# Fewer conversion steps in late slots, and another order of the integer additions, in a threshold-attention and GELU-MLP kernel

## The chip, the cores and the metric

The kernel runs on one core of one Trainium2 chip. The metric is the device time of one execution in microseconds, and the median over runs is what counts. Before the change it is 1330.39 us (three runs, 1327.67 to 1331.37).

## The reference

Attention runs over 8 batches of 8 heads, with 576 positions of 64 features, all in fp32. An MLP with exact GELU follows on the 4608 rows of 512.

```python
scores = scale * np.matmul(q, k.transpose(0, 1, 3, 2))
thresh = np.max(scores, axis=-1, keepdims=True) - tau
scores = np.where(scores >= thresh, scores, -1000000000.0)
scores = scores - np.max(scores, axis=-1, keepdims=True)
attn = np.exp(scores)
attn = attn / (np.sum(attn, axis=-1, keepdims=True) + 1e-09)
attn_out = np.matmul(attn, v)
# (B,H,S,D) -> (B*S, H*D)
h = x @ w_in                                      # 512 -> 2048
g = 0.5 * h * (1.0 + erf(h * inv_sqrt2))
out = g @ w_out                                   # 2048 -> 512
```

## The kernel before

Two heads form a pair; there are 32 pairs, four to a batch. The 576 rows of a head are cut into four chunks of 128 rows and a tail of 64. The tails of both heads of a pair share one chunk, chunk 4, which has one score tile instead of two. The main loop runs over slots `n`, each with one chunk `i` of one pair `p`. Slots 0 to 7 take chunks 0 and 1 of pairs 0 to 3. Slots 8 to 19 take chunks 2, 3 and 4 of these pairs in turn, so slots 10, 13, 16 and 19 are the one-chunk slots. From slot 20 on each pair has five slots in a row. Each engine's instructions run in the order in which the code issues them; semaphores between tiles do the rest.

A slot does this, for each head `e` of its pair:
- `scores` (L432, PE): scores into a PSUM tile `sc`, of which there are two buffers, so that the scores of the next slot wait until the last step below has read this slot's.
- `softmax_head`: the negated row maximum `nmx` (L444, DVE), the threshold `thr` (L447, GpSimd), and the exponential `p` (L449, ACT).
- `softmax_tail`: `p` where the score reaches the threshold, with the row sums (L465, DVE).
- Beside it PE does the transposes of `p` (L373), `weigh_v` (L603, L635) and, from slot 10, first steps of the MLP (L703).

While slots 1 to 21 run, the weights are rewritten. They come in 32 pieces of 128x512 words, 16 of `w_in` and 16 of `w_out`, and a pipeline of three engines converts each. `convert_first` takes two ACT instructions (L200, L201), one piece ahead. `convert_second` takes two DVE instructions, L208 (shift and mask) and L209 (sign bit), and then asks for the load of a later piece (L184, on the SP queue). `add_low_bits` takes one integer addition on GpSimd (L220), which makes the piece usable by PE. `STEPS[n]` says how many pieces slot `n` converts, at its end. Their additions are due in the next slot, at two places: one in `softmax_head`, after the first `nmx` is issued and ahead of `thr`, and the rest after `softmax_head`. In the kernel before, the first of these takes the newest of the sums that are due, and the second takes all that are left, oldest first.

The slot's other GpSimd work includes the divisions of early pairs. `divide_late` (L509, two multiplications) is issued in the slots that `DIVIDE_LATE` lists, behind the additions. At the end of slots 18 and 19 DVE transposes k and q of pair 4 (L410, L415) for the scores of slot 20. Slot 17 sets part of a `v` tile to zero on GpSimd (L256).

At the start, `load_early` loads q and k of pair 0: q from the SP queue and k from the ACT queue. `turn_qk_early(0)` has PE transpose them against an identity matrix into `tr` tiles, which ACT (q, with the scale; L327) and DVE (k of pair 0; L329) copy out. The tails have a tile of their own (L336, L341). For pair 0 the order is k, the tails, the first half of q and the second half of q. The scale `q_scale` is computed on DVE from `tau` (L1118 to L1122), and the memsets of the q tails and v tiles (L1129) follow it in DVE's order.

Of the kernel before, what the change touches and what calls it, by code (L numbers as in the profile page):

```python
# [8 lines left out]
FP32 = mybir.dt.float32  # L9
U32 = mybir.dt.uint32  # L10
U8 = mybir.dt.uint8
AF = mybir.ActivationFunctionType
# [6 lines left out]
def kernel(  # L19
# [28 lines left out]
    nc = tc.nc  # L48
    ctx.enter_context(tc.manual_schedule())

    B, H, S, D = q.shape
    d_model, d_ff = moe_w_in.shape
    P = 128
    Q = 32
    HP = H // 2
    NP = B * HP
    EARLY = HP
    NC = S // P
    MAIN = NC * P
    TAIL = S - MAIN  # L60
# [19 lines left out]
    ps = ctx.enter_context(tc.tile_pool(name="ps", bufs=4, space=PSUM))  # L80
# [40 lines left out]
    ident = const.tile([P, P], FP32, name="ident")  # L121
# [3 lines left out]
    q_tail = [att.tile([P, P], FP32, name=f"q_tail{i}") for i in range(4)]  # L125
    v_sb = [att.tile([P, 2, KR, D], FP32, name=f"v{i}") for i in range(4)]
# [11 lines left out]
    q_scale = const.tile([P, 1], FP32, name="q_scale")  # L138
# [7 lines left out]
    for _ in range(3):  # L146
# [4 lines left out]
    pieces = [(w_in_sb[c][:, f:f + PIECE], moe_w_in[c * P:(c + 1) * P, f:f + PIECE])  # L151
              for f in range(0, d_ff, PIECE) for c in range(N_DM)]
# [60 lines left out]

    sums_due = []

    def add_low_bits(newest=False):

        for _ in range(min(1, len(sums_due)) if newest else len(sums_due)):
            dst, power = sums_due.pop(-1 if newest else 0)
            nc.gpsimd.tensor_tensor(dst, power, dst, op=ALU.add)  # L220
            converted[0] += 1

# [42 lines left out]
    def load_early(p):  # L265
        b, hp = divmod(p, HP)
        s = st[p] = {}
        for name, src in (("q", q), ("k", k)):

            if p == 2:  # L270
                at = s[name + "_slot"] = x_slot()
                t = x_rows(at)[:, 0:2 * (NC + 1) * D].rearrange("p (e c d) -> p e c d", e=2, d=D)
            else:
                t = ld.tile([P, 2, NC + 1, D], FP32, tag=name, name=name)
            s[name] = t
            eng = (nc.scalar, nc.gpsimd)[p] if p < 2 and name == "k" else nc.sync
            for e in range(2):
                rows = src[b, 2 * hp + e, 0:MAIN, :]
                if name == "q":
                    eng.dma_start(t[:, e, 0:NC, :].rearrange("p (g c) d -> p g (c d)", c=2),  # L280
                                  rows.rearrange("(g p c) d -> p g (c d)", p=P, c=2))
                else:
                    eng.dma_start(t[:, e, 0:NC, :], rows.rearrange("(p t) d -> p t d", p=P))
            eng.dma_start(t[0:TAIL, :, NC, :], src[b, 2 * hp:2 * hp + 2, MAIN:S, :].rearrange("e s d -> s e d"))
# [15 lines left out]
    def turn_qk_early(p, names="qk"):  # L300


        s = st[p]
        if names == "k":
            qT, kT = s["qT"], s["kT"]
        elif 2 <= p < HP:
            qT = op.tile([P, MAIN], FP32, tag="o_sb", name="qT")
            kT = pd_tail[p - 2].rearrange("p b i -> p (b i)")
        else:
            qT = ld.tile([P, MAIN], FP32, tag="qT", name="qT")  # L310
            kT = ld.tile([P, TAIL + S], FP32, tag="kT", name="kT")
        s["qT"], s["kT"] = qT, kT
        qt = s["q_tail"] = q_tail[p % 4]
        copy = nc.scalar.copy if p else nc.vector.tensor_copy
        tiles = {name: s.pop(name) for name in names}

        def most(name, parts=1):
            t = tiles[name]
            tr = ps.tile([P, NC, P], FP32, tag="mm", name="tr")
            n = NC // parts  # L320
            for part in range(parts):
                for c in range(part * n, (part + 1) * n):
                    for e in range(2):
                        nc.tensor.matmul(tr[e * D:(e + 1) * D, c, :], lhsT=t[:, e, c, :], rhs=ident, start=True, stop=True)  # L324
                src = tr[:, part * n:(part + 1) * n, :].rearrange("p c s -> p (c s)")
                if name == "q":
                    nc.scalar.activation(qT[:, part * n * P:(part + 1) * n * P], src, AF.Copy, bias=0.0, scale=q_scale)  # L327
                else:
                    copy(kT[:, TAIL:S], src)  # L329

        def tails():
            tr = ps.tile([P, NC, P], FP32, tag="mm", name="tr")
            if "q" in names:
                none = q_tail[HP - 1][0:TAIL, D:2 * D]
                for e in range(2):
                    nc.tensor.matmul(tr[e * D:(e + 1) * D, 0, (1 - e) * TAIL:(2 - e) * TAIL], lhsT=ident[0:TAIL, 0:D],  # L336
                                     rhs=none, start=True, stop=True)
            for j, name in enumerate(names):
                for e in range(2):
                    at = e * TAIL if name == "q" else 0  # L340
                    nc.tensor.matmul(tr[e * D:(e + 1) * D, j, at:at + TAIL], lhsT=tiles[name][0:TAIL, e, NC, :],  # L341
                                     rhs=ident[0:TAIL, 0:TAIL], start=True, stop=True)
            if "k" in names:
                nc.scalar.copy(kT[:, S:S + TAIL], tr[:, j, 0:TAIL])
                nc.scalar.copy(kT[D:P, 0:TAIL], tr[D:P, j, 0:TAIL])
            if "q" in names:
                yield
                nc.scalar.activation(qt, tr[:, 0, :], AF.Copy, bias=0.0, scale=q_scale)

        if p == 0:  # L350
            most("k")
            rest = tails()
            next(rest)
            most("q", 2)
            next(rest, None)
            return
        for name in names:
            most(name)
        for _ in tails():
            pass  # L360
        x_free.extend(s.pop(name + "_slot") for name in names if name + "_slot" in s)

    def turn_p_early(p, i, later=None):

# [70 lines left out]
    def softmax_head(p, i):  # L435

        s = st[p]
        n = len(s["sc", i])
        nmx = small.tile([P, 2], FP32, tag="nmx", name="nmx")
        thr = s["thr", i] = small.tile([P, 2], FP32, tag="thr", name="thr")  # L440
        w = s["p", i] = work.tile([P, 2 * S], FP32, tag="p", name="p")
        for e in range(n):
            sc = s["sc", i][e][:, :, 0:HALF]
            nc.vector.tensor_reduce(nmx[:, e:e + 1], sc, axis=AXIS.XY, op=ALU.max, negate=True)  # L444
            if e == 0:
                add_low_bits(True)
            nc.gpsimd.tensor_scalar(  # L447
                thr[:, e:e + 1], nmx[:, e:e + 1], -1.0, tau_eff, op0=ALU.mult, op1=ALU.subtract)
            nc.scalar.activation(  # L449
                w[:, e * S:(e + 1) * S].rearrange("p (h s) -> p h s", h=2), sc, AF.Exp, bias=nmx[:, e:e + 1], scale=1.0)  # L450
# [663 lines left out]
        assert not beside  # L1114

    load_early(0)
    some = const.tile([P, 1], FP32, name="some")
    nc.vector.tensor_scalar(some, tau_sb, 0.0, None, op0=ALU.is_ge)  # L1118
    nc.vector.tensor_scalar(q_scale, some, SCALE, None, op0=ALU.mult)
# [5 lines left out]
    load_early(2)  # L1125
    for _ in range(4):
        load_piece(nc.sync)
    for t in q_tail + [t[:, :, NC, :] for t in v_sb]:
        nc.vector.memset(t, 0.0)  # L1129
    turn_qk_early(0)  # L1130
    load_v_early(0)
    load_early(3)
    load_v_early(1)

    parts = [(range(2), HP), (range(2, SLOTS), HP)] + [(range(SLOTS), 1)] * (NP - HP)
# [20 lines left out]

    PARTS = 1.3, 1.3, 0.2, 1.3, 0.9

    DIVIDE_LATE = {14: 0, 16: 1, 19: 2, 22: 3}
    STEPS = [0, 1, 1, 1, 1, 1, 1, 1, 1, 2, 2, 2, 3, 2, 2, 3, 3, 3, 1, 0, 1]  # L1160
    BUSY = {1: 2, 6: 2, 8: 2}

    tokens = 0
# [5 lines left out]
    for n in range(len(slots) + WEIGH + 1):  # L1169
        p, i = slots[n] if n < len(slots) else divmod(n, SLOTS)  # L1170
        early = p < EARLY
        last = slots[n - 1] if 0 < n <= len(slots) else None
        if p < NP:
            scores(p, i)
            softmax_head(p, i)
            add_low_bits()
            if last and last[0] < EARLY and last[1] < 2:
                invert(*last)
            if last and last[0] < EARLY and last[1] == NC:
                divisors_early(last[0])  # L1180
            if p == 0 and i == 0:
                turn_qk_early(1)
            elif p < HP - 1 and i < 2 and n > 1:
                turn_qk_early(p + 1, "qk"[i])
        elif n == len(slots):
            early_end.close()
            weights_first()
# [16 lines left out]
        if long:  # L1204
            convert_ahead(STEPS[n] - 1)
        if n in DIVIDE_LATE:
            divide_late(DIVIDE_LATE[n])
        if p > EARLY and i == WEIGH:
# [56 lines left out]
        elif n in (BATCH - 2, BATCH - 1):  # L1265
            turn_qk(HP, "k" if n == BATCH - 2 else "q")
        convert(STEPS[n] if n < len(STEPS) else 0)
        if not early:
# [58 lines left out]
```

## Time and profile before

| What | us |
|---|---|
| Median of three runs | 1330.39 |
| The profiled execution's own time | 1327.03 |
| Span of its trace | 1325.3 |
| PE busy in the span | 1313.4 |
| DVE busy | 1042.8 |
| GpSimd (POOL) busy | 634.2 |
| ACT busy | 601.9 |
| L208, 32 instructions: shortest, median, longest | 0.41, 0.42, 1.74 |
| L209, 32 instructions | 0.69, 0.69, 1.12 |
| L220, 32 instructions | 1.26, 1.27, 1.28 |

The profile is of one execution. An engine's busy time includes the time that an instruction is held inside the engine: a shift of 0.42 us that stands at 1.74 us has been held. Of PE's time one cannot read how fast it worked, only where it had nothing to do. The granted TensorE clock is 1.00 throughout. The span and the 1.73 us around it make the execution's own time.

### The profile page before, as it was taken

What the parts mean: (1) busy time and instruction counts of PE and PEld (TensorE: products, weight loads), DVE (VectorE), ACT (ScalarE), POOL (GpSimd) and SP (SyncE); (2) the same over time, 40 slices, a digit from 0 to 9 for tenths busy, and PEclk for the clock granted to TensorE, in tenths of its full rate; (3) what the DMA queues carried; (4) which work ended last, traced back from release to release, by engine and by line L of the source; (5) the groups of instructions that cost most, each with busy time, mean ns of one, the idle gap of its engine ahead of it and who ended that gap; (6) DMA issues with size and microseconds to landing.
All of it is one profiled execution on the core that took longest, in us unless ns stands there. A gap on an engine that the chain in (4) does not pass through costs nothing.

```text
span 1325.3 us, 19980 instructions
## 1 busy us (share of the span) xinstructions
PE 1313.4 (99%) x6362; PEld 890.3 (67%) x6362; DVE 1042.8 (79%) x2009; ACT 601.9 (45%) x1018; POOL 634.2 (48%) x1058
## 2 busy tenths in 40 slices
PE   9999999999999999999999999999999999999998
PEld 7775476576476466466466466478778787877877
DVE  6888877888888888888888888883857698386674
ACT  7888266376376367357457438232111203211120
POOL 3565555465555555565555541236364403645430
PEclk9999999999999999999999999999999999999999
DMA  8453676767777777787787775400000140000003
GB/s 256 161 178 106 145 164 159 166 156 168 189 164 164 191 181 165 193 190 168 184 192 170 176 165 115 100 9 0 1 1 0 40 110 11 0 1 0 1 0 80
DMA packets 213688, 153.14 MB, mean 116 GB/s; under 512 B 117264, under 2 KB 196992, under 8 KB 213584
## 3 DMA queue, kind: packets, MB, share of 16 engines
q1 hardware_dynamic: 195440, 125.31, 40.4%
q0 software_dynamic: 17712, 26.26, 7.5%
q8 instruction: 52, 0.85, 0.3%
q14 instruction: 52, 0.43, 0.1%
q10 hardware_dynamic: 432, 0.30, 0.1%
HBM read 56.62 MB, written 12.58 MB: 52 GB/s over the span
## 4 chain that ended last, share of the span: by engine, by line
PE 93%; DVE 2%; issue 1%; DMA 1%; ACT 1%; POOL 1%; SPq 0%; POOLq 0%; DVEq 0%; ACTq 0%
PE bank L891 34%; PE o_ps L718 17%; PE hT L703 16%; PE sc L432 13%; PE xT L603 11%; PE tr L373 1%; DVE nmx L444 1%; PE xT L635 1%; PE tr L324 1%; DVE power L209 1%; DVE power L208 0%; ACT p L449 0%; DVE p L465 0%; DMA inv<-turned 0%; DMA turned_p<-in_moe_w_out_dram 0%
## 5 line engine op out<-in xcount | busy, mean ns | idle before, releaser
L449 ACT ACTIVATE p<-sc,nmx 128x576 f32<-128x576 f32 x288 | 201.9, 737 | 280.0 <-DVE nmx L444 279.8
L465 DVE SCALAR_TENSOR_TENSOR p<-sc,thr,p 128x576 f32<-128x576 f32 x288 | 225.2, 815 | 70.6 <-ACT p L449 62.2
L447 POOL TENSOR_SCALAR thr<-nmx,tau_eff 128x1 f32<-128x1 f32 x288 | 83.9, 293 | 333.3 <-DVE nmx L444 331.2
L703 PE MATMUL hT<-xall,w_in 128*128 128x256 f32 x1024 | 241.8, 385 | 0.0
L444 DVE TENSOR_REDUCE nmx<-sc 128x1 f32<-128x576 f32 x288 | 205.4, 750 | 41.9 <-PE sc L432 40.7
L718 PE MATMUL o_ps<-w_out,g 128*128 128x512 f32 x512 | 236.8, 603 | 0.0
L703 PEld LDWEIGHTS hT<-xall,w_in 128*128 128x128 f32 x1024 | 189.4, 190 | 51.3 <-issue 24.0
L773 DVE TENSOR_TENSOR o<-o,bank 128x256 f32<-128x256 f32 (+1 forms) x242 | 100.1, 417 | 94.5 <-PE bank L891 89.5
L773 DVE TENSOR_TENSOR c<-c,bank 128x320 f32<-128x320 f32 x304 | 147.2, 487 | 33.7 <-PE bank L891 20.1
L718 PEld LDWEIGHTS o_ps<-w_out,g 128*128 128x128 f32 x512 | 93.1, 190 | 109.5 <-issue 107.2
L432 PE MATMUL sc<-kT,qT 64*128 64x288 f32 x960 | 160.1, 429 | 1.5 <-DVE p L465 1.4
L564 DVE STREAM_TRANSPOSE turned_p<-p 128x1152 f32<-128x1152 f32 x112 | 154.4, 1378 | 3.9
L603 PE MATMUL xT<-pT,v 128*64 128x320 f32 (+1 forms) x1200 | 153.6, 410 | 0.0
L432 PEld LDWEIGHTS sc<-kT,qT 64*128 64x128 f32 x960 | 91.2, 186 | 75.9 <-issue 61.1
L603 PEld LDWEIGHTS xT<-pT,v 128*64 128x64 f32 x1200 | 83.4, 137 | 68.0 <-issue 10.4
L891 PE MATMUL bank<-w_out,c 128*128 128x256 f32 (+1 forms) x484 | 120.5, 379 | 0.8 <-DVE o L773 0.8
L261 POOL DMA_DIRECT2D v<-in_v_dram x208 | 110.8, 536 | 3.6 <-issue 1.4
L891 PEld LDWEIGHTS bank<-w_out,c 128*128 128x128 f32 x484 | 90.3, 190 | 19.0 <-DVE o L773 3.2
L958 ACT ACTIVATE c<-c 128x320 f32<-128x320 f32 (+1 forms) x80 | 46.8, 623 | 114.7 <-DVE c L773 114.7
L773 POOL TENSOR_TENSOR c<-c,g 128x320 f32<-128x320 f32 (+1 forms) x40 | 50.5, 1271 | 67.5 <-DVE c L773 67.5
L891 PE MATMUL bank<-t_out,g 128*128 128x256 f32 (+1 forms) x324 | 82.4, 377 | 0.4 <-DVE o L773 0.4
L891 PE MATMUL bank<-t_out,c 128*128 128x256 f32 x320 | 82.7, 381 | 0.0
(188 smaller groups left out, 1755.9 us busy)
## 6 DMA issues: line engine op xcount, KB each, us to landing
pT<-turned_p SPq DMA_DIRECT2D x448, 160.0 KB, 3.5
pT<-pd_tail SPq DMA_DIRECT2D x112, 80.0 KB, 3.0
q<-in_q_dram POOLq DMA_DIRECT2D x104, 72.0 KB, 3.7
k<-in_k_dram POOLq DMA_DIRECT2D x104, 72.0 KB, 3.2
inv<-turned SPq DMA_DIRECT2D x54, 128.0 KB, 4.1
v<-in_v_dram POOLq DMA_DIRECT2D x156, 40.0 KB, 3.1
out_dram<-o SPq DMA_DIRECT2D x40, 128.0 KB, 2.4
xall<-in_moe_w_out_dram SPq DMA_DIRECT2D x9, 512.0 KB, 4.8
```

The lines of the kernel that those rows point to most:

```text
L261: eng.dma_start(t[r:P:4, e, 0:n, :], rows[:, r * KR:r * KR + n, :])
L432: nc.tensor.matmul(sc[e][:, h, 0:HALF], lhsT=lhsT, rhs=s["kT"][rows, at:at + HALF], start=True, stop=True)
L444: nc.vector.tensor_reduce(nmx[:, e:e + 1], sc, axis=AXIS.XY, op=ALU.max, negate=True)
L447: nc.gpsimd.tensor_scalar(thr[:, e:e + 1], nmx[:, e:e + 1], -1.0, tau_eff, op0=ALU.mult, op1=ALU.subtract)
L449: nc.scalar.activation(w[:, e * S:(e + 1) * S].rearrange("p (h s) -> p h s", h=2), sc, AF.Exp, bias=nmx[:, e:e + 1], scale=1.0)
L465: nc.vector.scalar_tensor_tensor(row, sc[e][:, :, 0:HALF], thr[:, e:e + 1], row, op0=ALU.is_ge, op1=ALU.mult, accum_out=den[e])
L564: nc.vector.transpose(turned_p[:, :, i // 2, 0:NB, i % 2 * Q:(i % 2 + 1) * Q], w.rearrange("p (e b i) -> p e b i", e=2, i=Q))
L603: nc.tensor.matmul(to, lhsT=s["v"][:, e, c, :], rhs=rhs, start=(c == 0), stop=(c == KR - 1))
L703: nc.tensor.matmul(hT[:, j % 2, :], lhsT=w_in_sb[c][:, j * P:(j + 1) * P], rhs=x_blk[n][:, c, :], start=(c == 0), stop=(c == N_DM - 1))
L718: nc.tensor.matmul(o[:, 0:d_model], lhsT=g[j][:, m * P:(m + 1) * P], rhs=w_out_sb[j], start=(j == 0), stop=(j == N_DF - 1))
L773: eng.tensor_tensor(out, a, b, op=ALU.add)
L891: nc.tensor.matmul(to, lhsT=l, rhs=r, start=start and k == 0, stop=k == len(pairs) - 1, skip_group_check=not start)
```

## The change

Four things change.
- `STEPS`: slots 16 and 17 convert two pieces instead of three, slots 18 and 19 two and one instead of one and none.
- `add_low_bits`: it takes the oldest sums first, at both places. After `softmax_head`, a one-chunk slot among the early ones takes one at most, so that such a slot has two in all; what is left goes to the next slot. 
- `DIVIDE_LATE`: the division of pair 1 is issued in slot 17 instead of 16.
- The start: pair 0 is transposed like the others, q whole, then k, then the tails, with q copied out in one instruction. The memsets of the q tails and v tiles come ahead of the computation of `q_scale`.

In the order of each engine's instructions, PE's changes only in the transposes of pair 0, and SP's not at all. DVE's changes at the start and from slot 16 to 20, ACT's at the start and from slot 17 to 20, and GpSimd's from slot 10 to 20.

```diff
-    def add_low_bits(newest=False):
+    def add_low_bits(most):
 
-        for _ in range(min(1, len(sums_due)) if newest else len(sums_due)):
-            dst, power = sums_due.pop(-1 if newest else 0)
+        for _ in range(min(most, len(sums_due))):
+            dst, power = sums_due.pop(0)
             nc.gpsimd.tensor_tensor(dst, power, dst, op=ALU.add)
             converted[0] += 1
...
             if e == 0:
-                add_low_bits(True)
+                add_low_bits(1)
...
-        if p == 0:
-            most("k")
-            rest = tails()
-            next(rest)
-            most("q", 2)
-            next(rest, None)
-            return
         for name in names:
-            most(name)
-        for _ in tails():
-            pass
+            t = s[name]
+            tr = ps.tile([P, NC, P], FP32, tag="mm", name="tr")
+            for c in range(NC):
                 for e in range(2):
+                    nc.tensor.matmul(tr[e * D:(e + 1) * D, c, :], lhsT=t[:, e, c, :], rhs=ident, start=True, stop=True)
+            src = tr.rearrange("p c s -> p (c s)")
+            if name == "q":
+                nc.scalar.activation(qT, src, AF.Copy, bias=0.0, scale=q_scale)
+            else:
+                copy(kT[:, TAIL:S], src)
...
     load_early(0)
+    for t in q_tail + [t[:, :, NC, :] for t in v_sb]:
+        nc.vector.memset(t, 0.0)
     some = const.tile([P, 1], FP32, name="some")
...
-    for t in q_tail + [t[:, :, NC, :] for t in v_sb]:
-        nc.vector.memset(t, 0.0)
     turn_qk_early(0)
...
-    DIVIDE_LATE = {14: 0, 16: 1, 19: 2, 22: 3}
-    STEPS = [0, 1, 1, 1, 1, 1, 1, 1, 1, 2, 2, 2, 3, 2, 2, 3, 3, 3, 1, 0, 1]
+    DIVIDE_LATE = {14: 0, 17: 1, 19: 2, 22: 3}
+    STEPS = [0, 1, 1, 1, 1, 1, 1, 1, 1, 2, 2, 2, 3, 2, 2, 3, 2, 2, 2, 1, 1]
...
             softmax_head(p, i)
-            add_low_bits()
+            add_low_bits(1 if early and i == NC else len(pieces))
```

## The prediction

> **What bounds the kernel now.** I read the table of busy time by stage first, to see where TensorE still has gaps, because an order of instructions can only win or lose there.
>
> ```profile
> 67.00:85.00 18.00, 17.57 (x101) 13.15 (x99) 15.10 (x30) 16.34 (x32) 10.00 (x15) 1.00 0.65 190
> 85.00:105.00 20.00, 18.45 (x103) 13.82 (x103) 17.84 (x34) 17.20 (x36) 12.90 (x18) 1.00 0.61 210
> ...
> 140.00:300.00 160.00, 159.97 (x773) 97.30 (x773) 130.13 (x232) 88.56 (x133) 81.71 (x167) 1.00 0.70 159
> 300.00:600.00 300.00, 300.00 (x1470) 180.03 (x1467) 262.18 (x472) 169.69 (x263) 167.24 (x339) 1.00 0.77 178
> ```
>
> The columns are the stretch, its length, then PE, PEld, DVE, ACT and POOL busy. From about 125 us PE has no gap. Before that DVE is busy 17.84 of 20 us and PE waits. So whatever the first 125 us (slots 0 to 20) gain or lose goes to the end almost one to one, and nothing later changes: the order of PE's instructions is the same in both kernels but for the first transposes, SP's is the same throughout.
>
> Next the timeline of slots 10 and 16, for what an addition (POOL L220) does to a conversion pair (DVE L208, L209).
>
> ```profile
> 57.07 0.69 DVE L209 SCALAR_TENSOR_TENSOR power<-xall,power 128x512 uint32<-128x512 uint32 x1
> ...
> 57.70 0.43 DVE L208 TENSOR_SCALAR power<-power 128x512 uint32<-128x512 uint32 x1
> ...
> 58.16 0.69 DVE L209 SCALAR_TENSOR_TENSOR power<-turned_p,power 128x512 uint32<-128x512 uint32 x1
> ...
> 58.77 0.75 DVE L444 TENSOR_REDUCE nmx<-sc 128x1 f32<-128x576 f32 x1
> 58.99 1.27 POOL L220 TENSOR_TENSOR w_in<-power,w_in 128x512 uint32<-128x512 uint32 x1 [2.25 <-DVE power L209]
> ```
>
> The head's addition takes the newest sum, so it starts 0.14 us after the last L209 (58.85) and lies under nmx.
>
> ```profile
> 96.67 2.50 POOL L220 TENSOR_TENSOR w_out<-power,w_out 128x512 uint32<-128x512 uint32 x2
> ...
> 97.95 1.51 DVE L208 TENSOR_SCALAR power<-power 128x512 uint32<-128x512 uint32 x1
> ...
> 99.13 1.65 POOL L509 TENSOR_TENSOR xall<-xall,w_out 128x256 f32<-128x256 f32 x2
> ...
> 99.49 1.11 DVE L209 SCALAR_TENSOR_TENSOR power<-xall,power 128x512 uint32<-128x512 uint32 x1
> ...
> 100.53 0.54 DVE L208 TENSOR_SCALAR power<-power 128x512 uint32<-128x512 uint32 x1
> ```
>
> Here two additions run into L208: it takes 1.51 us instead of 0.42 and ends 0.29 after them. Then L509, waiting since 99.13, goes ahead of L209 (1.11 instead of 0.69), and L208 follows. The two engines take turns.
>
> [...]
>
> **The change part by part.** A slot is one pass of the main loop; 10, 13, 16 and 19 are the one-chunk slots.
>
> *Order of the additions.* Now the head adds the oldest sum. With two or more conversions behind it this is ready 0.14 us after the first L209, while L208 of the second is running (it starts 0.06 before that L209 ends, and ends 0.36 after). The addition waits for it, takes the pair when it ends, as L509 did at 99.46, and the second L209, due at +0.40, is blocked. How long? L209 at 99.49 lost 0.42, so a 256-wide L509 (0.74 us) held the pair to about 99.93, some 0.47 us. The 512-wide addition takes 1.27, 0.53 more: a hold of 1.0 us. L209 starts at 1.36 instead of 0.40: **0.95 us per collision** (estimate). For it thr is no longer late (p waits for thr 0.3 to 0.4 us in slots 12, 15 and 18). What is queued behind the blocked L209 on DVE is nmx; ACT's exponential, p and PE's next scores wait for that in turn.
>
> *At most two additions in a one-chunk slot.* In slot 13, L208 at 79.32 (1.21 us, blocked by two additions) would be free: minus 0.8. But the third addition goes to the head of slot 14, is ready at once and meets the second L208: plus 1.0, of which a wait for ACT's L200 (81.4) covers part. Slot 14 has two additions instead of one after thr: plus 0.5, with the division behind them. The same in slots 16 and 17.
>
> *Conversions.* Slots 16 and 17 make two instead of three: minus 1.09 each (57.07 to 58.16, L209 to L209). Slots 18 and 19 make one more each: plus 1.09; in slot 18 this also makes a collision. ACT's L200/L201 (0.7 us each) move along and stay hidden: ACT waits for nmx in these slots. The pieces are all requested by slot 15, so no load moves past another on SP; loads come later by as much as their L209.
>
> *Division of pair one from slot 16 to 17.* L509 (0.74 and 0.32 us when free) no longer follows the additions at 99.13, minus 0.4 to 0.7 on DVE, and blocks the first pair of slot 17 instead, plus the same. On POOL it is now ahead of the memset of v and the head of slot 18. x of that pair is read long after.
>
> I walk the slots with these prices; the number is how much later nmx starts than before (estimates, each from the one above it):
> - 10: +0.95, one collision. 11: +1.4 (thr no longer holds p, −0.2; L208 at 61.31 is blocked 0.3 less; second collision).
> - 12: +2.2, third collision. 13: +2.0 (thr −0.2, fourth collision, but nmx had 0.75 of idle time before it, waiting for PE).
> - 14: +1.9 (L208 −0.8, the leftover +0.9, less waiting for ACT). PE's scores of slot 15, which had waited 0.71 us for p, start 1.9 late.
> - 15: +3.75 (one addition more before L208 and L509 with it, +0.9, then a collision). 16: +4.1 (a collision, less 0.27 of idle time and thr's 0.3).
> - 17: +2.0 (its L208 and L209 free of one addition and of L509, −1.8; one pair less, −1.1; the leftover, +0.95). PE's scores of slot 18 start 2.0 late.
> - 18: +2.1 (L509 and a collision against one pair less and shorter blocking of L208).
> - 19: +3.4 (p +1.9, L208 at 114.56 blocked 0.4 less, one pair more with its collision, +2.0).
> - Scores of slot 20 wait for qT (L415, 118.57), behind p of slot 19: **+3.3**. PE has no gap soon after, so this goes to the end.
>
> *q first, memsets first.* The chain of waits at the start is k transposes (to 6.15), tails, half q (6.96), ACT 0.47, half q again (8.12: the buffer waits for ACT), scores 8.71. After: q from about 4.4 (its loads take 3.0 us from issue at 0.75 and 1.24, so land by 4.3; PE's idle matmuls end at 4.24), to 6.2; k 1.05 more; tails 0.6 (as at 11.77); two ACT copies of 0.21; scores at 8.3 to 8.5. Between minus 0.4 and plus 0.2 (if q lands later); I take **minus 0.3**. The memsets (1.2 us of DVE) move into the wait for tau (3.57 us), which hides them; the transposes no longer wait 0.35 for q_tail. POOL's building of ident runs beside them, and PE is busy until 4.24.
>
> Sum: +3.3 − 0.3 = **+3.0 us**. The profiled execution took 1327.03 (span 1325.3 and 1.73 around it), which gives 1330.0. The median of the runs shown, 1330.39, is 3.4 above that execution, so I forecast 1330.4 + 3.0 = **1333.4**. What a measurement can tell from no change is 0.3%, 4.0 us.
>
> **Rivals.**
> - *VectorE keeps the pair between its own instructions.* Then the additions fall behind the last L209 as before and only the reliefs stay. Slot 16: one pair less (1.09), one addition less before L208; PE's scores of slot 18 could start at once after its transposes, 103.9 instead of 105.57; slot 18's extra pair gives little back. About −1.5, with the start −1.8: 1328.6. Against it: L509 overtook L209 at 99.49. For it: this is a single clear case, and there L208 had just been served.
> - *Each collision costs the whole addition, so the kernel is slower.* If an addition holds the pair for its 1.27 us and is taken up 0.14 later, a collision costs 1.35. Eight of them lie ahead of slot 17, 0.4 more each is 3.2: +6, 1336.4. It decides from a hold of about 1.15 us on, where the sum passes 4.0. For it: no L209 of this trace stands against a whole addition; the hold is carried over from a narrower operation. Against: L208 at 79.32 ends 0.29 after the additions, too soon for a pair that is free only when their span is over, since L208 takes 0.42.
> - *The moves cancel*: PE's own work (hT in slots 12 to 18) hides more than I count, and the total is within 1 us: 1330.4. The order of instructions shows that the moves really take place, so it cannot be that nothing happens.
>
> **How the numbers follow.** The forecast, taking turns at 1.0 us, 0.52, with its own range of +1 to +5; VectorE keeps the pair 0.15; the dearer collision 0.25; cancelled 0.08. Slower by over 0.3%: a third of the first (0.18) and nearly all of the dearer case (0.24): 0.42. Faster by over 0.3%: 0.02. The rest, 0.56, is within. The range runs from VectorE keeping the pair (1328.6 less a little scatter) to the dearer case with 1.6 more: 1328.4 to 1338.0; without rivals it would be 1331.4 to 1335.4.
>
> **What would show it.** In the profile after, one L220 should start between the two L209 of slots 9 to 12, and the second L209 should take about 1.6 us instead of 0.69: mean of L209 up from 0.70, nmx of slot 10 about 0.95 late, scores of slot 18 near 107.3 and of slot 20 near 122.5. If L209 stays at 0.69 everywhere I am wrong on the port; if scores of slot 20 are on time, on the slack; if the first scores come after 8.71, on the start.

## The result, and the profile after

The kernel after takes 1330.54 us (median of 14 runs, 1328.79 to 1335.10). The kernel before took 1328.22 us beside it (14 runs, 1326.60 to 1331.37). The ratio is **1.0021, 95% interval [1.0011, 1.0031]**, or 2.8 us more (1.5 to 4.1). This is less than the 0.3% that the prediction took as the least that can be told from no change, and close to its +3.0 us (3.0 / 1330.4 = 0.23%). The forecast of 1333.4 us itself was 2.9 us too high, because it stood on the median of three runs, 1330.39, where 14 runs of the same kernel give 1328.22. In the text below, all differences in us of timed runs are such a ratio times 1328.2.

First the table by stage of the kernel after, with the columns as before: stretch, length, PE, PEld, DVE, ACT, POOL, granted clock, DMA share, GB/s.

```profile
67.00:85.00 18.00, 17.66 (x101) 13.13 (x99) 15.73 (x28) 15.17 (x31) 8.57 (x12) 1.00 0.65 183
85.00:105.00 20.00, 18.20 (x99) 13.24 (x97) 18.42 (x32) 15.70 (x33) 12.46 (x14) 1.00 0.66 218
...
140.00:300.00 160.00, 159.97 (x767) 97.11 (x768) 130.06 (x235) 86.67 (x131) 82.53 (x169) 1.00 0.73 161
300.00:600.00 300.00, 300.00 (x1471) 180.00 (x1468) 262.22 (x470) 169.96 (x260) 167.47 (x340) 1.00 0.78 178
```

DVE is busy 15.73 us instead of 15.10 in the first stretch and 18.42 instead of 17.84 in the second, with fewer instructions (28 and 32 instead of 30 and 34): something holds them. From 140 us on PE is full in both kernels, so what was lost before is kept.

The timeline of slot 10 shows what holds it (start, duration, engine, line, operation). Lines have moved up by some 18; nmx is L426 now, scores L414, thr L429.

```profile
55.91 0.69 DVE L209 SCALAR_TENSOR_TENSOR power<-xall,power 128x512 uint32<-128x512 uint32 x1
...
56.53 0.43 DVE L208 TENSOR_SCALAR power<-power 128x512 uint32<-128x512 uint32 x1
56.68 1.42 POOL L220 TENSOR_TENSOR w_in<-power,w_in 128x512 uint32<-128x512 uint32 x1 [1.09 <-DVE power L209]
...
57.00 1.65 DVE L209 SCALAR_TENSOR_TENSOR power<-turned_p,power 128x512 uint32<-128x512 uint32 x1
...
58.57 0.74 DVE L426 TENSOR_REDUCE nmx<-sc 128x1 f32<-128x576 f32 x1
```

The addition of the first sum is released at 56.68 by the first L209, while L208 of the second piece runs. L208 ends at 56.96. The addition goes first, and the second L209 takes 1.65 us instead of 0.69. If 0.69 of that is its own work, it was held until 58.65 - 0.69 = 57.96, 1.00 us after L208 ended. "The port" (in the prediction also "the pair" that an engine holds, takes or keeps) is a name for what DVE and GpSimd hold in turn: the traces show which engine waited and for how long, not what in the chip it waited for. So reckoned, the addition of 128x512 held the port for 1.00 us, although its span here is 1.42 us and lasts 0.14 us beyond the release.

The groups of DVE instructions of the kernel after (busy time, mean ns):

```profile
L209 DVE SCALAR_TENSOR_TENSOR power<-turned_p,power 128x512 uint32<-128x512 uint32 x15 | 15.6, 1040 | 0.5
L209 DVE SCALAR_TENSOR_TENSOR power<-xall,power 128x512 uint32<-128x512 uint32 x17 | 14.1, 830 | 0.6
```

The two groups had 692 and 717 ns before. Seven of the 32 L209 take 1.64 or 1.65 us, two 1.11 us, all others 0.69 or 0.70.

In slot 14, after the division that was not moved, both kinds of meeting follow each other:

```profile
87.87 1.65 POOL L491 TENSOR_TENSOR xall<-xall,w_out 128x256 f32<-128x256 f32 x2
...
88.22 1.11 DVE L209 SCALAR_TENSOR_TENSOR power<-turned_p,power 128x512 uint32<-128x512 uint32 x1
...
89.26 0.54 DVE L208 TENSOR_SCALAR power<-power 128x512 uint32<-128x512 uint32 x1
89.48 1.45 POOL L220 TENSOR_TENSOR w_out<-power,w_out 128x512 uint32<-128x512 uint32 x1
89.83 1.65 DVE L209 SCALAR_TENSOR_TENSOR power<-xall,power 128x512 uint32<-128x512 uint32 x1
```

L491 (the division, L509 before) has two instructions. The first goes ahead of L209 (1.11), the second ahead of L208 (0.54), and the addition ahead of the next L209 (1.65): three times in a row the two engines take turns.

The start, PE with what follows it, kernel after:

```profile
4.16 1.57 PE L320 MATMUL tr<-ident,q 128*64 128x128 f32 x15
...
5.57 1.14 PE L320 MATMUL tr<-ident,k 128*64 128x128 f32 x15
...
7.59 1.38 PE L414 MATMUL sc<-kT,qT 64*128 64x288 f32 x8 [0.38 <-DVE kT L325]
```

The first scores start at 7.59 instead of 8.71, 1.12 us earlier. The experiments show that this one execution is the earliest of ten.

### The profile page after: what moved, and what is told of

The parts are those of the page before. It is cut to its first block, busy times and chain, and to the rows that moved or that the text cites. A ratio compares the mean times of both kernels' runs of the same rounds, so it can differ in the third digit from the quotient of the medians.

```text
span 1327.8 us, 19982 instructions
## 1 busy us (share of the span) xinstructions
PE 1313.9 (99%) x6362; PEld 890.3 (67%) x6362; DVE 1048.2 (79%) x2009; ACT 601.4 (45%) x1017; POOL 637.2 (48%) x1058
## 3 DMA queue, kind: packets, MB, share of 16 engines
q1 hardware_dynamic: 195440, 125.31, 40.7%
## 4 chain that ended last, share of the span: by engine, by line
PE 92%; DVE 3%; DMA 1%; issue 1%; ACT 1%; SPq 0%; POOL 0%; DVEq 0%; POOLq 0%; ACTq 0%
PE bank L873 34%; PE o_ps L700 17%; PE hT L685 15%; PE sc L414 13%; PE xT L585 10%; DVE power L209 1%; DVE nmx L426 1%; DVE power L208 1%; PE tr L320 1%; PE tr L355 1%; PE xT L617 1%; DVE p L447 1%; ACT p L431 1%; DMA inv<-turned 0%; DMA turned<-turned 0%
## 5 line engine op out<-in xcount | busy, mean ns | idle before, releaser
L429 POOL TENSOR_SCALAR thr<-nmx,tau_eff 128x1 f32<-128x1 f32 x288 | 84.0, 293 | 345.9 <-DVE nmx L426 343.9
L426 DVE TENSOR_REDUCE nmx<-sc 128x1 f32<-128x576 f32 x288 | 205.2, 749 | 38.4 <-PE sc L414 37.2
L414 PE MATMUL sc<-kT,qT 64*128 64x288 f32 x960 | 160.4, 429 | 3.6 <-DVE p L447 2.9
L414 PEld LDWEIGHTS sc<-kT,qT 64*128 64x128 f32 x960 | 91.6, 186 | 77.9 <-issue 62.9
```

Of the source, the lines that this page charges most:

```text
L414: nc.tensor.matmul(sc[e][:, h, 0:HALF], lhsT=lhsT, rhs=s["kT"][rows, at:at + HALF], start=True, stop=True)
L429: nc.gpsimd.tensor_scalar(thr[:, e:e + 1], nmx[:, e:e + 1], -1.0, tau_eff, op0=ALU.mult, op1=ALU.subtract)
```

## The experiments

"The new start" means the fourth part of the change: q whole, then k, then the tails, and the memsets first. To compare traces I take the start of the scores of slot 20, from where PE has nearly no gap, minus the start of the first scores, so that the start of an execution drops out. This **distance** is 119.47 - 8.71 = 110.76 us before and 121.16 - 7.59 = 113.57 us after: +2.81. From the scores of slot 20 to the end the fourteen profiles take 1205.3 to 1207.7 us, so the time of a single execution can differ from what its distance says by some 2 us.

Unless a number is given, a timed kernel has 13 or 14 runs, with 26 to 43 runs of the kernel before beside it (medians 1327.97 to 1328.29 us).

### The new start alone

```diff
 # the kernel after, with all but the new start put back as before
-    DIVIDE_LATE = {14: 0, 17: 1, 19: 2, 22: 3}
+    DIVIDE_LATE = {14: 0, 16: 1, 19: 2, 22: 3}
...
-            add_low_bits(1 if early and i == NC else len(pieces))
+            add_low_bits()
```

> The kernel before with the new start alone (q first and whole, memsets first). Theory (the profiles' reading): the first scores start at 7.6 instead of 8.7 us and all later slots by 1.1 us earlier, the end too: 1.1 us less than before. Rival: a later slot waits for loads that are not earlier, and takes it back: 0 to 0.3 us less, with nmx of slot 10 at 58.8 as before.

Measured: 1327.37 us, ratio 0.9988 [0.9977, 0.9999], so -1.6 us (-3.1 to -0.1). In its profile the first scores start at 8.63, hardly before those of the kernel before, and the distance is 111.77. The timeline of PE shows why it is not 110.76:

```profile
105.17 2.68 PE L414 MATMUL sc<-pd_tail,qT 64*128 64x288 f32 x8 [1.54 <-DVE p L447]
```

PE had waited 1.54 us for p, and then eight score matmuls take 2.68 us instead of the usual 1.94: the granted clock fell. The mean granted clock is 0.56 from 106 to 108 us and 0.59 from 108 to 110 us. This returns below. The new start gains, but one profile doesn't show by how much.

### Oldest first alone

```diff
-            dst, power = sums_due.pop(-1 if newest else 0)
+            dst, power = sums_due.pop(0)
```

> The kernel before with the oldest sum first in the head, nothing else. Theory (collisions of the head's addition with the second L209 are the cost): L209 of 1.65 us in the slots with two or more pieces, scores of slot 20 about 3 to 4 us later, the kernel 3 to 4 us slower than before. Rival (the moved conversion steps are the cost): L209 may be long, but PE's own work hides it, within 1 us of before.

Measured: 1336.86 us (5 runs), ratio 1.0059 [1.0046, 1.0072], +7.8 us, more than expected. Its profile has eight L209 of 1.65 us. It also has two spells of low clock (0.50 from 94 to 96 us and from 114 to 118 us), after waits of PE of 1.75 us (scores of slot 15) and 2.55 us (scores of slot 18); the second in the timeline of PE:

```profile
113.36 2.99 PE L432 MATMUL sc<-pd_tail,qT 64*128 64x288 f32 x8 [2.55 <-DVE p L465]
116.29 4.67 PE L603 MATMUL xT<-pT,v 128*64 128x320 f32 x20
```

The 20 matmuls of xT take 4.67 us; in the kernel after, at full clock, 2.91 (88.15). Scores and xT together lose 1.05 + 1.76 = 2.8 us. Over its five runs the mean clock is 0.9952, against 0.9986 of the kernel before. The profile also starts late, with first scores at 9.78, so I ran the same order with the new start as well (below).

### The kernel after with the newest first in the head

```diff
-            dst, power = sums_due.pop(0)
+            dst, power = sums_due.pop(-1 if newest else 0)
...
-                add_low_bits(1)
+                add_low_bits(1, True)
```

> The changed kernel, but the head takes the newest sum as before the change. Theory (collisions are the cost): no L209 of 1.65 us, some 3 to 4 us less than the changed kernel, 1 to 2.5 us less than before. Rival (the moved conversion steps are the cost): 2 to 3 us slower than before, like the changed kernel.

Measured: 1326.40 us (12 runs), ratio **0.9983 [0.9975, 0.9991]**: this beats both kernels. Its timeline of slot 10:

```profile
57.64 0.43 DVE L208 TENSOR_SCALAR power<-power 128x512 uint32<-128x512 uint32 x1
...
58.10 0.69 DVE L209 SCALAR_TENSOR_TENSOR power<-turned_p,power 128x512 uint32<-128x512 uint32 x1
58.71 0.75 DVE L426 TENSOR_REDUCE nmx<-sc 128x1 f32<-128x576 f32 x1
58.94 1.27 POOL L220 TENSOR_TENSOR w_in<-power,w_in 128x512 uint32<-128x512 uint32 x1 [2.23 <-DVE power L209]
```

The second L209 is back at 0.69 us, and the addition lies under nmx. No L209 of this kernel takes more than 1.12 us. The distance is 109.15, 4.42 us below the kernel after. Neither trace has a spell of low clock between 10 and 130 us (1.00 in every stretch). The order of one addition per slot is therefore worth 4.4 us in the traces and (1.0021 - 0.9983) x 1328.2 = 5.0 us in the times. Seven collisions of 0.96 us make 6.7, so about a third of them doesn't reach slot 20. One part of that third: with the oldest first p waits less for thr, 1.8 us in all between 12 and 70 us instead of 2.9.

### A memset in place of the head's addition

In the head the addition is left out, and GpSimd sets its `power` tile to zero instead; the sums of those pieces are missing.

```diff
+            if head:
+                nc.gpsimd.memset(power, 0)
+            else:
                 nc.gpsimd.tensor_tensor(dst, power, dst, op=ALU.add)
```

> The changed kernel with a memset of the same 128x512 words (the power tile) in place of the head's addition; those pieces lack their sum, so this part of the weights' conversion is left out. The memset waits for the same L209 and writes, but reads nothing. [...] Rival (anything that GpSimd runs there blocks L209, or L209 waits for something else): L209 over 1.0 us again in these slots.

One run, 1325.49 us. Its timeline of slot 10:

```profile
57.42 0.43 DVE L208 TENSOR_SCALAR power<-power 128x512 uint32<-128x512 uint32 x1
57.56 0.75 POOL L221 MEMSET power<- 128x512 uint32 x1 [1.07 <-DVE power L209]
57.88 0.69 DVE L209 SCALAR_TENSOR_TENSOR power<-turned_p,power 128x512 uint32<-128x512 uint32 x1
```

The memset starts in the same place, 0.06 us after the end of the first L209 (0.08 for the addition), and the second L209 doesn't wait. In slots 11 and 12 the memset starts just ahead of L208 and makes that 0.80 and 0.76 us long instead of 0.42, while the L209 behind it stay at 0.69. A memset is shorter than an addition (0.53 us in slot 11), but a wait of that length would show. So it is not any work of GpSimd's that blocks L209 here: beside the memset, which reads nothing, L209 takes 0.69 us, and beside the addition, which reads two tiles, 1.65. That the addition's reads make this difference is my estimate; no run varies them, or the inputs of L209.

### The new start with the new steps and division

The head adds the newest, and there is no cap.

```diff
 # the new start alone, and
-    DIVIDE_LATE = {14: 0, 16: 1, 19: 2, 22: 3}
-    STEPS = [0, 1, 1, 1, 1, 1, 1, 1, 1, 2, 2, 2, 3, 2, 2, 3, 3, 3, 1, 0, 1]
+    DIVIDE_LATE = {14: 0, 17: 1, 19: 2, 22: 3}
+    STEPS = [0, 1, 1, 1, 1, 1, 1, 1, 1, 2, 2, 2, 3, 2, 2, 3, 2, 2, 2, 1, 1]
```

> The new start together with the new STEPS and DIVIDE_LATE; the head still adds the newest sum and the one-chunk slots add all. Theory (the moved conversions relieve slots 16 and 17): scores of slot 18 start about 1.5 us earlier, relative to the first scores, than with the new start alone, and about 1 us of that is left at slot 20, so the time is about 1.2 us below the new start alone: ratio to before 0.9983. Rival (slots 18 and 19 give the two pairs back, and what the newest-first kernel with all moves gained came from the cap): as the new start alone, 0.9988.

Measured: 1325.92 us (22 runs), ratio **0.9983 [0.9976, 0.9989]**, as expected. But the rival's 0.9988 lies in this interval too, so the times alone don't tell whether steps and division gain anything. The traces do. The distance is 116.69 - 7.86 = 108.83, 1.93 below the kernel before. Counted from the first scores, nmx of slot 18 starts 3.29 us earlier than before, and nmx of slot 20 1.93 us earlier: the moved conversions do relieve slots 16 and 17, and only a part is given back in 18 and 19. Scores of slot 18 start at 103.10 instead of 105.57, 1.62 us earlier from the first scores. PE's wait ahead of the scores of slot 18, 1.81 us before, is 0.26 us here:

```profile
103.10 1.94 PE L414 MATMUL sc<-pd_tail,qT 64*128 64x288 f32 x8 [0.26 <-DVE p L447]
```

### The new start with the cap alone

```diff
 # the new start alone, and
-            add_low_bits()
+            add_low_bits(most=1 if early and i == NC else 99)
```

> The new start together with the cap alone: the end of a one-chunk slot adds one sum instead of all; the head adds the newest, STEPS and DIVIDE_LATE as before. Theory (with the newest first, the head's leftovers meet no L209, so the cap only takes an addition out of the way of L208 in slots 13 and 16): L208 of 1.21 us in slot 13 and 1.51 us in slot 16 shorten by 0.4 to 0.8, the time is 0.3 to 0.8 us below the new start alone: ratio to before 0.9984. Rival (the leftover addition comes back in the next slot at full price): 0.9988 or above.

Measured: 1328.34 us, ratio 1.0006 [0.9997, 1.0014]; the rival was right. In slot 13 L208 does shorten to 0.42 us. But with three conversions in slots 16 and 17 the sums that are left over pile up. Timeline of slot 17 in this kernel:

```profile
104.04 3.92 POOL L220 TENSOR_TENSOR w_out<-power,w_out 128x512 uint32<-128x512 uint32 x3
...
105.33 1.49 DVE L208 TENSOR_SCALAR power<-power 128x512 uint32<-128x512 uint32 x1
...
106.86 1.65 DVE L209 SCALAR_TENSOR_TENSOR power<-turned_p,power 128x512 uint32<-128x512 uint32 x1
```

Three additions in a row block L208 (1.49) and then L209 (1.65). With the new steps the pile is smaller: the kernel with everything but oldest first (0.9983) stands where steps and division alone stand (0.9983). So the cap gains nothing in either pair of kernels that differ in it alone; with the oldest first it wasn't run alone.

### The kernel after with additions in halves

```diff
-            nc.gpsimd.tensor_tensor(dst, power, dst, op=ALU.add)
+            for h in range(2):
+                half = slice(h * PIECE // 2, (h + 1) * PIECE // 2)
+                nc.gpsimd.tensor_tensor(dst[:, half], power[:, half], dst[:, half], op=ALU.add)
```

> The kernel after, with each addition L220 split in two of 256 columns. Theory (the engines take turns, instruction by instruction): the first half goes ahead of the second L209 and holds the port for about 0.5 us, then L209 runs and the second half waits for it: the L209 of 1.65 us become about 1.15, seven of them give 7 x 0.5 = 3.5 us less delay in the slots, of which some half reaches the end as with the other changes: ratio to before 1.0005 to 1.001 instead of 1.0021. Rival (GpSimd keeps the port from one instruction to the next): L209 stays at 1.6 or more, ratio 1.002 or more.

Measured: 1327.31 us, ratio **0.9996 [0.9987, 1.0006]**. The gain over the kernel after is 3.3 us, more than was expected. Timeline of slot 10:

```profile
58.01 0.43 DVE L208 TENSOR_SCALAR power<-power 128x512 uint32<-128x512 uint32 x1
58.17 1.99 POOL L222 TENSOR_TENSOR w_in<-power,w_in 128x256 uint32<-128x256 uint32 x2 [1.08 <-DVE power L209]
...
58.47 1.10 DVE L209 SCALAR_TENSOR_TENSOR power<-turned_p,power 128x512 uint32<-128x512 uint32 x1
```

All additions of the same sum in the same place, cut in two: L209 takes 1.10 us instead of 1.65, so it waited for one half (0.41) and not for both. GpSimd's second half was next in its queue, and still L209 went between: it came free at 58.88, and the second half starts by the trace at 58.99. So GpSimd doesn't keep the port from one instruction to the next here. A port that goes to whichever engine is asking when it comes free would give the same lines as taking turns; the runs don't tell these two apart.

### Oldest first with the new start

```diff
 # the new start alone, and
-            dst, power = sums_due.pop(-1 if newest else 0)
+            dst, power = sums_due.pop(0)
```

> The new start together with the oldest sum first in the head; no cap, STEPS and DIVIDE_LATE as before. Theory (oldest first by itself costs about 8 us in this schedule, as the kernel with it alone showed, and the other moves give half of it back): ratio to before about 1.0052, that is 1.0059 less the start. Rival (the late start of that kernel's profile was part of its time, and oldest first costs the 4 us of eight collisions at most): 1.002 to 1.003.

Measured: 1331.40 us (7 runs), ratio 1.0033 [1.0021, 1.0046], between the two expectations and nearer to the rival's. Against the new start alone, oldest first costs (1.0033 - 0.9988) x 1328.2 = 6.0 us with the old steps; with the new steps and the cap it was 5.0. The distance is 125.31 - 8.34 = 116.97, +6.21. The eight L209 of 1.65 us explain a part; the rest is in PE's stretches from 84 to 100 us (columns as above, the clock is third from the end):

```profile
84.00:88.00 4.00, 2.27 (x13) 1.83 (x12) 3.97 (x8) 2.63 (x6) 2.33 (x4) 1.00 0.64 219
88.00:94.00 6.00, 5.98 (x22) 2.76 (x23) 5.72 (x9) 4.52 (x10) 3.63 (x7) 0.53 0.61 191
```

and in its timeline of PE:

```profile
87.76 3.00 PE L414 MATMUL sc<-pd_tail,qT 64*128 64x288 f32 x8 [1.73 <-DVE p L447]
90.68 5.15 PE L585 MATMUL xT<-pT,v 128*64 128x320 f32 x20
```

PE waited 1.73 us for p, which collisions had made late, and then ran for 6 us at 0.53 of its clock: scores 3.00 us instead of 1.94, xT 5.15 instead of 2.91, 3.3 us in all. nmx of slot 15 is still 3.72 us late relative to the start, as the collisions make it; nmx of slot 16, behind these matmuls, is 6.12 late. So oldest first costs about 4 us by the collisions here, and some 2 us more by the clock of 0.53 behind the wait of 1.73 us. The timed runs agree: the mean clock of these seven is 0.9974, that of the new start alone 0.9987, and 0.0013 of 1328 us is 1.7 us (estimate). For oldest first alone (0.9952 against 0.9986) the same estimate gives 0.0034 x 1328 = 4.5 of its 7.8 us. In the kernel after, the longest wait of PE between 60 and 125 us is 1.04 us, and its clock stays at 1.00. So steps, division and cap together keep PE's waits short in that kernel; how much each of them does for it with the oldest first was not run.

### The memsets first, alone, and the order of the transposes, alone

The memsets alone:

```diff
     load_early(0)
+    for t in q_tail + [t[:, :, NC, :] for t in v_sb]:
+        nc.vector.memset(t, 0.0)
...
-    for t in q_tail + [t[:, :, NC, :] for t in v_sb]:
-        nc.vector.memset(t, 0.0)
     turn_qk_early(0)
```

> The kernel before with the memsets of the tails moved ahead and nothing else. Theory (the transposes of the tails no longer wait 0.35 us for q_tail, and VectorE has room while tau is on its way): first scores 0.2 to 0.35 us earlier than with the old start in the same pace of TensorE, ratio to before 0.9995 to 1.0. Rival (the memsets come between TensorE's warm-up operand and the first transposes, and set the start back): ratio 1.0005 or more.

Measured: 1327.60 us, ratio 0.9994 [0.9984, 1.0004]: not told apart from nothing. Its first scores start at 9.25, and this says little about the memsets: the transposes of q's tail had to wait for q until 6.68, and the granted clock is 0.50 from 8.42 to 11.83 us, so that the second half of q takes 1.03 us instead of 0.66.

The order of the transposes alone, which is `turn_qk_early` as in the change with the memsets left where they were:

```diff
-        if p == 0:
-            most("k")
...
         for name in names:
+            t = s[name]
```

> The kernel before with the new order of the first transposes (q whole, then k, then the tails) and nothing else; the memsets stay late. Theory (q in halves made TensorE wait 0.57 us for ACT, which goes; the tails' wait for the memsets is hidden behind k): most of the start's gain, ratio to before 0.999, first scores near 8.4. Rival (q comes later from memory than k, so the transposes start later): first scores at 8.7 or later, ratio 1.0 or more.

Measured: 1327.19 us (22 runs), ratio 0.9986 [0.9977, 0.9994], first scores at 8.29: as far as the times can tell, the order of the transposes has all of the start's gain. Its distance is 110.48.

### Steps, newest first, additions in halves

```diff
 # the new start with the new steps and division, and
-            nc.gpsimd.tensor_tensor(dst, power, dst, op=ALU.add)
+            for h in range(2):
+                half = slice(h * PIECE // 2, (h + 1) * PIECE // 2)
+                nc.gpsimd.tensor_tensor(dst[:, half], power[:, half], dst[:, half], op=ALU.add)
```

> The kernel with the new start and the new STEPS and DIVIDE_LATE, newest sum first, with each addition L220 split in two of 256 columns. Theory (a half holds the port for 0.5 us instead of 1.0): the L208 of 1.2 us in slot 13 and the L209 of 1.65 us in slot 16 shorten to about 1.0 and 1.1, in all 0.5 to 1 us, of which part reaches the end: ratio to before 0.9976 to 0.9982. Rival (two instructions for one keep VectorE waiting more often, since GpSimd has twice as many turns): 0.9985 or more.

Measured: 1327.17 us, ratio 0.9993 [0.9983, 1.0004], above the 0.9983 of whole additions; the rival's outcome came true. The two intervals overlap, but the distance agrees: 118.46 - 8.32 = 110.14, 1.31 more than with whole additions. Timeline of slot 16:

```profile
97.58 3.41 POOL L222 TENSOR_TENSOR w_out<-power,w_out 128x256 uint32<-128x256 uint32 x4
...
98.39 0.88 DVE L208 TENSOR_SCALAR power<-power 128x512 uint32<-128x512 uint32 x1
...
99.31 1.10 DVE L209 SCALAR_TENSOR_TENSOR power<-xall,power 128x512 uint32<-128x512 uint32 x1
```

L208 (0.88) and L209 (1.10) lose 0.87 us together here, where with whole additions they lose 1.09 (0.55 and 1.65): not much is saved. Over all 32 pieces L208 and L209 lose 3.6 us with halves and 3.7 us with whole additions: one long wait of L209 has become four short ones. And something is paid elsewhere. The waits of VectorE between 12 and 70 us, with total, number and longest, first with whole additions:

```profile
DVE p L447 <- POOL thr L429: 2.9, 7, 1.1
```

then with halves:

```profile
DVE p L449 <- POOL thr L431: 4.8, 10, 1.2
```

Two halves take 1.41 us on GpSimd where one whole addition takes 1.27, and thr stands behind them, so p waits longer for it. By slot 13, counted from the first scores, nmx is 0.73 us later than with whole additions, though until then L208 and L209 have lost no more than there. So what is lost goes with GpSimd's own time rather than with the number of turns. The kernel after with halves pays this too and gains all the same, since there the halves shorten seven collisions.

### The kernel before again

> The kernel before once more, for its profile: how far the first scores move from one execution to the next without any change. Theory (the start depends on the pace at which TensorE's first transposes run, which differs between executions): first scores anywhere between 8.5 and 9.8 us, the L209 of 1.11 us in slot 16 at the same distance from them as before or taken in another turn. Rival (the start is fixed by the program): 8.7.

Measured: one run, 1327.37 us, first scores at 8.59, distance 119.35 - 8.59 = 110.76, as in the first profile of this kernel. The L209 of 1.11 us in slot 16 is there again. So in these two profiles, whose clock is 1.00 in every stretch from 10 to 130 us, the schedule behind the first scores repeats, while the start moved by 0.12.

The starts differ with the pace of PE's first transposes. PE in the kernel after with the newest first, which has the start of the kernel after:

```profile
4.17 2.37 PE L320 MATMUL tr<-ident,q 128*64 128x128 f32 x15
...
6.33 1.50 PE L320 MATMUL tr<-ident,k 128*64 128x128 f32 x15
...
8.70 1.38 PE L414 MATMUL sc<-kT,qT 64*128 64x288 f32 x8 [0.38 <-DVE kT L325]
```

The same 15 transposes start at the same time and take 2.37 us instead of 1.57, those of k 1.50 instead of 1.14, and the scores are 1.11 us later. The records of the granted clock in the traces begin with full clock, at 4.89 us in the kernel after and at 7.04 us here; what the clock was before that they don't show. (Where a trace has no record yet, the tables show 1.00; so the 1.00 throughout that is given for the kernel before holds from 6.62 us to 1324.17 us.) Over ten profiles with the new order of transposes this record begins between 4.89 and 7.37 us, and the first scores start between 7.59 and 8.78 (middle 8.33): the later the one, the later the other, but for one pair of neighbours. Over four profiles with the old order the first scores start between 8.59 and 9.78 (middle 8.98). The two latest of these are oldest first alone, where the record begins only at 14.07 us and each half of q takes 1.12 us instead of 0.66, and the memsets alone, where the clock is 0.50 from 8.42 to 11.83.

## Why the prediction was right

**The collision.** Mechanism and size held. The prediction took 0.95 us per collision from a hold of 1.0 us, scaled from a half-width multiplication; the trace shows 0.96 us and a hold of 1.00. Reading what DVE lost, and not POOL's span of 1.27 or 1.42 us, made this possible. The predicted hold of a 256-wide instruction was 0.47 us (its own lines, 99.49 + 0.42 - 99.46, give 0.45); the kernel with halves shows 0.44 us by the same working, from the end of L208 at 58.44 to 59.57 - 0.69 = 58.88.

**The walk.** How much later nmx starts than before, relative to the first scores (1.12 us is added to each difference of the two traces):

| Slot | 10 | 11 | 12 | 13 | 14 | 15 | 16 | 17 | 18 | 19 | scores of 20 |
|---|---|---|---|---|---|---|---|---|---|---|---|
| predicted | 0.95 | 1.4 | 2.2 | 2.0 | 1.9 | 3.75 | 4.1 | 2.0 | 2.1 | 3.4 | 3.3 |
| trace | 0.92 | 1.39 | 2.35 | 2.28 | 2.26 | 4.07 | 4.49 | 2.59 | 1.57 | 3.01 | 2.81 |

Every value is right within 0.6 us. The prediction had leftovers meeting L209 in slots 14 and 17; in the trace they meet L208, which then takes 0.94 (at 82.06) and 1.19 us (at 102.40). That is 0.5 and 0.8 us instead of 0.95.

**The start** is the step whose size is least sure. Predicted were -0.3 us and -0.4 at most, with scores at 8.3 to 8.5. The middle of the ten profiles, 8.33, is in that span. The 8.71 from which the step subtracted was at the early end for the old order, but a like comparison gives the predicted size: in that profile the record of full clock begins at 6.62, and the two profiles of the new order that are nearest to it, at 6.49 and 6.50, have their first scores at 8.34 and 8.46, 0.25 to 0.37 us earlier. The times give more: -1.6 us for the new start (-3.1 to -0.1, which still takes in -0.3) and -1.9 for the order of the transposes alone (-3.1 to -0.8, which doesn't). The profiles account for 8.98 - 8.33 = 0.65 us, and the shorter distance, 110.48 instead of 110.76, for 0.28 more; together 0.93 us, inside both intervals, though 8.98 is the middle of four profiles, two of them the late ones above. The rest isn't settled. A clock that falls less often may be a part of it: the mean clock of the 22 runs with the order alone is 0.9990, that of the 43 runs of the kernel before 0.9984, and 0.0006 of 1328 us is 0.8 us (estimate).

**The clock** is in no step of the prediction. It did not need it for the kernel after, where PE waits 1.04 us at most between 60 and 125 us and the clock is 1.00, but it bears on what its parts are worth: oldest first with the new start but without the moves loses some 2 us more than its collisions explain, at a clock of 0.53 from 88 to 94 us.

**The sum.** The total was met at +2.8 against +3.0. How much of this closeness is luck stays open. By the traces neither step is far off: the walk gave 2.8 instead of 3.3, and the start gained some 0.3 us more than predicted. By the times two errors of over 1 us cancel: the start gave -1.6 instead of -0.3, and the rest cost 2.8 + 1.6 = 4.4 us instead of 3.3. The interval of the start is 1.5 us to each side, too wide to decide.

**The rivals.** VectorE didn't keep the port: seven times a whole addition went ahead of L209, though L209 started only 0.04 us after L208 had ended (56.96 and 57.00 in slot 10). The dearer collision (1.35 us, 1336.4) is ruled out by the hold of 1.00. That the moves cancel was not far off by time, but for another reason: a loss of 5 us by the order of the additions and gains of 2.3 us by start, steps and division.

## What to carry to other kernels

Where two engines hold each other up, as DVE and GpSimd do here, and both have work queued, ask of each instruction what will be waiting when the one ahead of it ends; an instruction that becomes ready a moment too early can overtake one on the critical path. Here the addition was released 0.28 us before L208 ended, and the L209 behind it took 1.65 us instead of 0.69. To size such a wait, take what the blocked instruction lost, not the span of the one that blocks it. A change in several parts can hide a gain: here the start and the moved steps together gain 2.3 us, and the order of one addition per slot costs twice that. And a wait of the bounding engine can cost more than its length, where its clock falls behind it: behind one wait of 1.73 us the matmuls lost 3.3 us at 0.53 of the clock. Look at the granted clock after each long wait.

## What the hardware showed that was not expected

DVE and GpSimd, where both have work queued, alternate instruction by instruction in the lines with additions shown here: L209 goes from 0.69 to 1.65 us behind a whole addition and to 1.10 behind a half one, with the other half next in GpSimd's queue.

TensorE's granted clock fell to 0.50 behind a wait of only 1.54 us. In the fourteen profiles, nine waits of PE of 1.53 us or more lie between 80 and 125 us, all ahead of scores; a spell at half clock follows four of them (1.54, 1.73, 1.75 and 2.55 us) and none follows the others (1.53, 1.68, 1.80, 1.81 and 1.82 us). In this stretch no wait of 1.25 us or less is followed by one.

In these profiles the four waits that are hit fall elsewhere in the record of the clock than the five others. From the first record of full clock to the end of the trace, the clock in the fourteen profiles changes only at whole steps of 3.413 us: stretches at full clock last 1 to 387 steps (386 in the first profile of the kernel before, 387 in the kernel after), spells at half clock one or two. How the steps lie to the program differs from one execution to the next; in the two profiles of the kernel before they begin at 6.62 and 5.77 us. The four spells begin at the end of a step; the waits behind which they come begin 0.27 us before that step (1.75) or at most 1.16 us into it. The five other waits begin 1.34 to 2.27 us into theirs. Here are the step with the wait and the next one, with the new start alone (hit) and with the order of the transposes alone (not hit); columns as above:

```profile
102.82:106.23 3.41, 1.85 (x12) 1.12 (x12) 3.34 (x9) 3.02 (x9) 3.41 (x5) 1.00 0.60 235
106.23:109.64 3.41, 3.41 (x14) 1.62 (x12) 3.31 (x6) 3.41 (x7) 0.90 (x2) 0.50 0.15 30
...
101.89:105.30 3.41, 1.88 (x12) 1.34 (x10) 3.33 (x8) 3.08 (x8) 3.01 (x5) 1.00 0.57 226
105.30:108.71 3.41, 3.39 (x24) 1.81 (x24) 3.34 (x6) 3.37 (x7) 1.51 (x3) 1.00 0.13 29
```

PE is busy for 1.85 and 1.88 us of the first step, and for 1.16 to 1.91 us of the steps ahead of the four spells, so the busy time alone doesn't decide. These nine waits were sorted after the fact, and no run moved a wait within the steps on purpose, so a rule by place isn't shown. Nor did the half clock always follow one long wait: with the memsets first, at the start, that from 8.42 us follows a step in which PE was busy for 2.16 us and its longest wait was 0.66 us.
